# Six row buffers for P, a later output projection and earlier loads of the second group's weights in a fused attention and gMLP kernel

## The chip, the cores and the metric

The kernel runs on one core of one Trainium2 chip. The metric is the device time of one execution in microseconds (us); of several executions the median is given.

## The reference, cut to what matters

```python
# x: 2048 x 512; 32 query heads of 128, 8 key/value heads (groups) of 2048 keys; bf16
h = layernorm(x) * (1 + ca) + sa                     # sa, ca, ga, ... from silu(c) @ w_mod
q = (h @ wq)                                         # per group: 4 heads share one k and v
p = softmax(q @ k.T / sqrt(128)); o = p @ v
x = x + ga * (o @ wo)                                # output projection, summed over the groups
# then a second layernorm and a gMLP block (not touched by the change)
```

## The kernel before

The attention is cut into 128 **units**: 16 query tiles of 128 rows for each of 8 groups, four heads each. **Iteration** n computes the scores of unit n in eight slots (two 128x512 matmuls and one exponential of 128x1024 each), and beside them in the same slots the product with V (PV) of an earlier unit, the query projection of a later block and the output projection of a still earlier unit. In this way TensorE always has work while ScalarE computes exponentials.

Units come in two forms. "By columns": scores come out with keys on the partitions, so P is at once what PV wants. "By rows" (every second unit from 8 to 120): scores come out with queries on the partitions, ScalarE sums the rows as it goes, VectorE scales them, and P goes through a DMA transpose on the Sync queue into the place where PV, three iterations later, reads it. Each of the four heads of such a unit has one row buffer of 4 KB per partition, used again by the next unit by rows, two iterations later.

```python
    pn = [win_t[:, r * SK : (r + 1) * SK] for r in range(REP - 1)]
    pn.append(wmod_a[:].rearrange("p k n -> p (k n)")[:, 0:SK])   # the fourth row buffer
    ...
    TURN_A, TURN_B = 2 * CT, NU - CT - 2                # 8 and 122

    def by_rows(u):
        return TURN_A <= u < TURN_B and u % 2 == 0

    def pv_at(u):
        return u + 3 if by_rows(u) else u + 1
    ...
            nc.scalar.activation(                        # in qk(u, i): hh, half = divmod(i, 2)
                out=pn[hh][:, half * HK : (half + 1) * HK], in_=s_ps[:], func=ACT.Exp,
                scale=inv_sqrt_dh, accum_out=rsums[u][:, i : i + 1],
            )
    ...
    def turn_rows(u, hh):
        ...                                              # tot = sum of the two halves; rinv = 1 / tot
        nc.vector.tensor_scalar(out=pn[hh], in0=pn[hh], scalar1=rinv, scalar2=None, op0=ALU.mult)
        nc.sync.dma_start_transpose(out=pTs[u][:, :, hh * P : (hh + 1) * P], in_=pn[hh])
```

The output oT of a unit by columns goes through a DMA transpose too, on the same Sync queue, and the output projection reads it two iterations after PV. The loads of a group's weights stand in the order of the GpSimd queue. The slot given with `at` sets only that order: an instruction goes out as soon as the queue reaches it and its buffers are free, which can be many iterations ahead of its slot.

```python
    for g in range(1, HKV):
        it = (g - 1) * NT
        at(it + 7, 4, lambda g=g: load_wq(g, nc.gpsimd))
        at(it + 9, 5, lambda g=g: load_k(g))             # a DMA transpose from DRAM, on Sync
        at(it + 11, 4, lambda g=g: load_v(g))
        at(it + 13, 4, lambda g=g: load_wo(g, nc.gpsimd))
    ...
        wos = [u for u in (it - 7, it - 5, it - 3) if 0 <= u < NU and pv_at(u) + 2 == it]
```

## Time and profile before

| | kernel before |
|---|---|
| time, median of the first 3 runs | 1315.53 us (1315.16 to 1317.28) |
| span in the profile | 1313.5 us |
| TensorE busy | 1293.9 us, 99% |
| ScalarE busy | 1109.7 us, 84% |

The prediction works out what bounds this kernel and where TensorE waits.

### The profile page before, as it was taken

The page shows a single profiled execution, that of the slowest core. Times are in us where ns is not written, and L with a number is a line of the kernel's source. Part 1 is how long each engine was busy: PE and PEld are TensorE (multiplying, and loading weights), DVE is VectorE, ACT ScalarE, POOL GpSimd, SP SyncE. Part 2 cuts the span into 40 slices and gives each one's busy share as a digit, 9 for nine tenths or more (in the row PEclk, how much of TensorE's full clock was granted, in tenths as well). Part 3 has the DMA queues.
Part 4 walks back from the last instruction along what each step waited for, and adds up shares of the span by engine and source line. Part 5 has one row for each costly group of instructions (what it writes and reads, how often), then busy time and mean ns, then how long its engine had stood idle before and what let it go on. Part 6 is the DMA issues. An engine that isn't in the chain of part 4 may idle for free.

```text
span 1313.5 us, 24523 instructions
## 1 busy us (share of the span) xinstructions
PE 1293.9 (99%) x9452; PEld 740.6 (56%) x9623; DVE 683.1 (52%) x1675; ACT 1109.7 (84%) x1517; POOL 53.9 (4%) x96
## 2 busy tenths in 40 slices
PE   9999999999999999999999999999999999999998
PEld 5665555555555555555555555555555556644445
DVE  6644454444455544445454544444555686784444
ACT  7899999999999999999999999999999998650000
POOL 1110000000000000000000000000000011120000
PEclk9999999999999999999999999999999999999999
DMA  6479787978777777778786868687766673264300
GB/s 181 106 119 187 127 154 127 150 135 154 151 145 145 135 145 141 140 140 165 136 157 124 160 124 157 130 156 149 147 126 127 122 135 85 52 140 99 75 20 27
DMA packets 592172, 170.53 MB, mean 130 GB/s; under 512 B 581712, under 2 KB 588112, under 8 KB 592048
## 3 DMA queue, kind: packets, MB, share of 16 engines
q1 hardware_dynamic: 585024, 149.74, 62.3%
q0 software_dynamic: 4432, 16.91, 4.6%
q10 hardware_dynamic: 2592, 2.23, 0.5%
q8 instruction: 77, 1.26, 0.4%
q14 instruction: 47, 0.39, 0.1%
HBM read 21.89 MB, written 2.10 MB: 18 GB/s over the span
## 4 chain that ended last, share of the span: by engine, by line
PE 97%; DMA 1%; issue 1%; DVE 0%; ACT 0%; ACTq 0%; DVEq 0%
PE o_ps L1076 20%; PE s_ps L1020 19%; PE s_ps L1001 15%; PE o_ps L1055 15%; PE misc L1108 8%; PE misc L944 8%; PE misc L1433 7%; PE s_ps L1267 2%; PE s_ps L1306 2%; PE o_ps L1454 1%; DMA wsp<-wmod_a 1%; PE s_ps L1454 0%; DMA wmod_a<-in_w_mod_dram 0%; PE misc L854 0%; PE o_ps L785 0%
## 5 line engine op out<-in xcount | busy, mean ns | idle before, releaser
L1027 ACT ACTIVATE pT<-s_ps 128x1024 bf16<-128x1024 f32 x560 | 567.9, 1025 | 33.1 <-PE s_ps L1020 10.4
L1076 PEld LDWEIGHTS <-pT 128*128 128x128 bf16 x4480 | 299.5, 98 | 130.8
L1008 ACT ACTIVATE win_sb<-s_ps 128x1024 bf16<-128x1024 f32 x342 | 349.9, 1024 | 7.4 <-PE s_ps L1001 1.1
L1076 PE MATMUL o_ps<-v,pT 128*128 128x129 bf16 x4480 | 344.9, 220 | 1.2
L1020 PE MATMUL s_ps<-qT,kT 128*128 128x512 bf16 x1136 | 337.8, 379 | 2.9 <-ACT wmod_a L1008 1.3
L1001 PE MATMUL s_ps<-kT,qT 128*128 128x512 bf16 x889 | 266.5, 379 | 3.0
L1108 PE MATMUL misc<-wo_g,oT 128*128 128x512 bf16 x465 | 176.5, 380 | 1.7 <-DMA oT<-onorm 1.1
L1020 PEld LDWEIGHTS <-kT 128*128 128x128 bf16 x1136 | 110.1, 98 | 115.9 <-issue 4.5
L944 PE MATMUL misc<-hT,wq_g 128*128 128x512 bf16 (+2 forms) x480 | 172.7, 371 | 0.8
L1055 PEld LDWEIGHTS <-v 128*128 128x128 bf16 x912 | 89.2, 98 | 107.6
L955 DVE CAST qT<-misc 128x512 bf16<-128x512 f32 x125 | 85.7, 686 | 120.7 <-PE misc L944 120.6
L1064 DVE CAST oT<-o_ps 128x512 bf16<-128x512 f32 x57 | 39.4, 692 | 191.7 <-PE o_ps L1055 154.6
L1055 PE MATMUL o_ps<-wsp,v 128*128 128x512 bf16 x442 | 132.7, 379 | 0.6
L1042 DVE TENSOR_SCALAR win_sb<-win_sb,rall 128x2048 bf16<-128x2048 bf16 x171 | 128.8, 753 | 6.2 <-DVE rall L1041 0.3
L1055 PE MATMUL o_ps<-pT,v 128*128 128x512 bf16 x426 | 128.6, 379 | 0.6
L1001 PEld LDWEIGHTS <-qT 128*128 128x128 bf16 x912 | 89.1, 98 | 60.1 <-issue 0.2
L1008 ACT ACTIVATE wmod_a<-s_ps 128x1024 bf16<-128x1024 f32 x114 | 116.6, 1023 | 2.6 <-DMA wsp<-wmod_a 1.3
L1038 DVE TENSOR_TENSOR tot<-rs 128x1 f32<-128x1 f32 x228 | 35.2, 154 | 132.8 <-ACT win_sb L1008 131.6
L1433 PE MATMUL misc<-wsp,z 128*128 128x512 bf16 (+2 forms) x554 | 100.4, 336 | 0.5 <-issue 0.2
L1433 PEld LDWEIGHTS <-z 128*128 128x128 bf16 x560 | 50.6, 98 | 48.5
L1121 DVE TENSOR_TENSOR xacc<-misc,xacc 128x512 f32<-128x512 f32 x112 | 76.2, 680 | 0.0
L944 PEld LDWEIGHTS <-wq_g 128*128 128x128 bf16 x528 | 50.4, 98 | 29.3 <-issue 0.4
(107 smaller groups left out, 734.5 us busy)
## 6 DMA issues: line engine op xcount, KB each, us to landing
wq_g<-in_A_wq_dram POOLq DMA_DIRECT2D x7, 512.0 KB, 6.3
v<-in_A_v_cache_dram POOLq DMA_DIRECT2D x7, 512.0 KB, 6.2
wo_g<-in_A_wo_dram POOLq DMA_DIRECT2D x7, 512.0 KB, 4.3
wsp<-in_w_mod_dram POOLq DMA_DIRECT2D x1, 2048.0 KB, 10.3
out_dram<-yout ACTq DMA_DIRECT2D x16, 128.0 KB, 1.7
win_sb<-in_B_w_in_dram POOLq DMA_DIRECT2D x1, 1792.0 KB, 7.9
x_sb<-in_A_x_dram SPq DMA_DIRECT2D x3, 512.0 KB, 5.7
wsp<-win_sb SPq DMA_TRANSPOSE x87, 4.4
```

Of the source, the lines that this page charges most:

```text
L944: nc.tensor.matmul(ps[0][:, o0 : o0 + n], lhsT=wqs[g][:, dt, hh * DH : (hh + 1) * DH], rhs=hTs[ch][:, dt, c0 : c0 + n], start=(dt == 0), s ...
L955: nc.vector.tensor_copy(out=dst, in_=src)
L1001: nc.tensor.matmul(s_ps[:, c * 512 : (c + 1) * 512], lhsT=qTs[b][:, hh, jj * P : (jj + 1) * P], rhs=groups[g]["kT"][:, k0 : k0 + 512], sta ...
L1008: nc.scalar.activation(out=pn[hh][:, half * HK : (half + 1) * HK], in_=s_ps[:], func=ACT.Exp, scale=inv_sqrt_dh, accum_out=rsums[u][:, i : ...
L1020: nc.tensor.matmul(s_ps[:, h * 512 : (h + 1) * 512].rearrange("p (r q) -> p r q", r=REP), lhsT=groups[g]["kT"][:, kt * P : (kt + 1) * P], ...
L1027: nc.scalar.activation(out=pTs[u][:, 2 * i : 2 * i + 2, :], in_=s_ps[:].rearrange("p (k q) -> p k q", k=2), func=ACT.Exp, scale=inv_sqrt_dh,)
L1042: nc.vector.tensor_scalar(out=pn[hh], in0=pn[hh], scalar1=rinv, scalar2=None, op0=ALU.mult)
L1055: nc.tensor.matmul(o_pss[u][:], lhsT=groups[g]["v1"][:, kt, 0:DH], rhs=pTs[u][:, kt, :], start=(kt == 0), stop=(kt == NKT - 1),)
L1076: nc.tensor.matmul(o_ps[:, hh % 2, 0 : DH + 1], lhsT=pTs[u][:, kt, hh * P : (hh + 1) * P], rhs=groups[g]["v1"][:, kt, 0 : DH + 1], start=( ...
L1108: nc.tensor.matmul(X_ps[:], lhsT=oTs[u][:, hh, :], rhs=groups[g]["wo"][:, hh, :], start=(hh == 0), stop=(hh == REP - 1),)
L1121: nc.vector.tensor_tensor(out=xaccs[j][:], in0=X_ps[:], in1=xaccs[j][:], op=ALU.add)
L1433: nc.tensor.matmul(g_ps[:, :n], lhsT=z2[:, st, f * P : (f + 1) * P], rhs=wsp[t][:, st, c0 : c0 + n], start=(st == 0), stop=(st == NT - 1 a ...
```

## The change

Its intent: P by rows shall find a free buffer (a ring of six in place of four); the projection shall not wait for oT (one iteration later for units 8 to 121, with five oT buffers in place of three); and the loads for group 1 shall be out of the way before the transposes of P begin (at slot 2 of iteration 5, ahead of the modulation rows, which go to DRAM and back and behind which they stood).

```diff
--- before.py
+++ after.py
@@ -659,6 +659,7 @@
 
     pn = [win_t[:, r * SK : (r + 1) * SK] for r in range(REP - 1)]
     pn.append(wmod_a[:].rearrange("p k n -> p (k n)")[:, 0:SK])
+    pn += [early.tile([P, SK], BF16, name=f"pn{k}", bufs=1) for k in range(2)]
     wmod_b = wspp.tile([P, NDT * 4 * D], BF16, name="wsp")[:].rearrange(
         "p (k n) -> p k n", k=NDT
     )
@@ -731,7 +732,7 @@
             nc.sync.dma_start(
                 out=v1[:, NKT // 2 : NKT, 0:DH], in_=v_dram[:, 0, NKT // 2 : NKT]
             )
-        groups[g]["v1"] = v1
+        groups.setdefault(g, {})["v1"] = v1
 
     def load_wo(g, engine):
         wo_g = late.tile([P, REP, D], BF16, name="wo_g")
@@ -741,7 +742,7 @@
     def load_k(g):
         kT = early.tile([P, SK], BF16, name="kT")
         nc.sync.dma_start_transpose(out=kT[:], in_=A_k_cache[0, g])
-        groups[g] = dict(kT=kT)
+        groups.setdefault(g, {})["kT"] = kT
 
     nc.gpsimd.memset(mhalf[:], -0.5)
     make_identity(nc, ident[:])
@@ -970,6 +971,9 @@
     def pv_at(u):
         return u + 3 if by_rows(u) else u + 1
 
+    def wo_at(u):
+        return pv_at(u) + (3 if TURN_A <= u < TURN_B else 2)
+
 
     users, homes = dict(pT0=-2, pT1=-1, wsp=CT + 2), {}
     for u in range(NU):
@@ -1006,7 +1010,7 @@
                     stop=True,
                 )
             nc.scalar.activation(
-                out=pn[hh][:, half * HK : (half + 1) * HK],
+                out=rows_of(u, hh)[:, half * HK : (half + 1) * HK],
                 in_=s_ps[:],
                 func=ACT.Exp,
                 scale=inv_sqrt_dh,
@@ -1031,6 +1035,9 @@
             scale=inv_sqrt_dh,
         )
 
+    def rows_of(u, hh):
+        return pn[((u - TURN_A) // 2 * REP + hh) % len(pn)][:, 0:SK]
+
     def turn_rows(u, hh):
         c0 = u * REP + hh
         rs, rinv = rsums[u], rall[:, c0 : c0 + 1]
@@ -1039,12 +1046,9 @@
             out=tot[:], in0=rs[:, 2 * hh : 2 * hh + 1], in1=rs[:, 2 * hh + 1 : 2 * hh + 2], op=ALU.add
         )
         nc.vector.reciprocal(out=rinv, in_=tot[:])
-        nc.vector.tensor_scalar(
-            out=pn[hh], in0=pn[hh], scalar1=rinv, scalar2=None, op0=ALU.mult
-        )
-        nc.sync.dma_start_transpose(
-            out=pTs[u][:, :, hh * P : (hh + 1) * P], in_=pn[hh]
-        )
+        rows = rows_of(u, hh)
+        nc.vector.tensor_scalar(out=rows, in0=rows, scalar1=rinv, scalar2=None, op0=ALU.mult)
+        nc.sync.dma_start_transpose(out=pTs[u][:, :, hh * P : (hh + 1) * P], in_=rows)
 
     def pv_rows(u, i, n):
 
@@ -1060,7 +1064,7 @@
                 stop=(kt == NKT - 1),
             )
         if i == n - 1:
-            oTs[u] = late.tile([P, REP, P], BF16, name="oT", bufs=3)
+            oTs[u] = late.tile([P, REP, P], BF16, name="oT", bufs=5)
             nc.vector.tensor_copy(
                 out=oTs[u][:], in_=o_pss[u][:].rearrange("p (r q) -> p r q", r=REP)
             )
@@ -1092,7 +1096,7 @@
                 op=ALU.mult,
             )
         if i == NSLOT - 1:
-            oTs[u] = late.tile([P, REP, P], BF16, name="oT", bufs=3)
+            oTs[u] = late.tile([P, REP, P], BF16, name="oT", bufs=5)
             nc.sync.dma_start_transpose(
                 out=oTs[u][:], in_=onorms[u][:].rearrange("p r d -> p (r d)")
             )
@@ -1250,10 +1254,10 @@
         at(NU + 1 + st // 4, 2 * (st % 4), lambda st=st: load_wsp(wsp[0], 0, st))
     for g in range(1, HKV):
         it = (g - 1) * NT
-        at(it + 7, 4, lambda g=g: load_wq(g, nc.gpsimd))
         at(it + 9, 5, lambda g=g: load_k(g))
-        at(it + 11, 4, lambda g=g: load_v(g))
-        at(it + 13, 4, lambda g=g: load_wo(g, nc.gpsimd))
+        at(*((5, 2) if g == 1 else (it + 7, 4)), lambda g=g: load_wq(g, nc.gpsimd))
+        at(*((5, 2) if g == 1 else (it + 11, 4)), lambda g=g: load_v(g))
+        at(*((5, 2) if g == 1 else (it + 13, 4)), lambda g=g: load_wo(g, nc.gpsimd))
 
 
     zs = {}
@@ -1356,7 +1360,7 @@
             z2p = fast.enter_context(tc.tile_pool(name="z2p", bufs=1))
             zs["z2"] = z2p.tile([P, NT, FH], BF16, name="z2")
         pvs = [u for u in (it - 5, it - 3, it - 1) if 0 <= u < NU and pv_at(u) == it]
-        wos = [u for u in (it - 7, it - 5, it - 3) if 0 <= u < NU and pv_at(u) + 2 == it]
+        wos = [u for u in range(max(it - 6, 0), min(it - 2, NU)) if wo_at(u) == it]
         wf = [fn for u in wos for fn in wo_proj(u)]
         for i in range(NSLOT):
             for fn in later.pop((it, i), []):
```

## The prediction

> **What bounds the kernel now.** The first thing read was the busy shares and, with them, the shares of the chain that ended last.
>
> ```profile
> PE 1293.9 (99%) x9452; PEld 740.6 (56%) x9623; DVE 683.1 (52%) x1675; ACT 1109.7 (84%) x1517; POOL 53.9 (4%) x96
> PE 97%; DMA 1%; issue 1%; DVE 0%; ACT 0%; ACTq 0%; DVEq 0%
> ```
>
> TensorE is busy for 1293.9 of 1313.5 us and is 97% of the chain. A busy TensorE may still be idling inside its matmuls, so I checked the step from one matmul to the next. In the middle of the attention, two 128x512 matmuls start every 0.43 us, 216 ns each, and eight 128x129 ones take 0.46 us, 57 ns each. That is the rate of a pipeline that never waits. I then took, for every pair of neighbouring matmuls in the whole trace, the distance of their starts less the usual step of that shape (a distance that is one whole step too long is a missing record and left out). The excess, by stretch, is 2.9 us in the first 20 us, 3.5 us from 80 to 120 us, 0.7 us from 260 to 280 us, 1.9 us after 1300 us, and below 0.2 us in each other stretch of 20 us; 7.6 us in all after small negative terms. The change touches neither the start nor the end of the program, so it can win at most 3.5 + 0.7 = 4.2 us of 1315.5. The view of busy time by stretch shows the same two places, 1.8 us short and 0.5 us short of their neighbours:
>
> ```profile
> 100.00:120.00 20.00, 18.00 (x135) 10.06 (x136) 7.60 (x21) 17.66 (x30) 0.00 (x0) 1.00 1.07 199
> 120.00:140.00 20.00, 19.84 (x157) 11.75 (x158) 10.64 (x28) 19.56 (x31) 0.00 (x0) 1.00 0.77 120
> ...
> 260.00:280.00 20.00, 19.31 (x145) 11.10 (x146) 10.30 (x27) 18.58 (x29) 0.00 (x0) 1.00 0.74 131
> ```
>
> The columns after the length are busy us of TensorE, weight loads, VectorE, ScalarE, GpSimd, then the clock, the DMA share and GB/s. The DMA share of 1.07 beside 0.77 says what is special about the first place. The timeline there, in order of time:
>
> ```profile
> 81.86 0.76 POOL L720 DMA_DIRECT2D wq_g<-in_A_wq_dram  x1
> 82.75 1.18 POOL L728 DMA_DIRECT2D v<-in_A_v_cache_dram  x1
> 83.90 0.78 POOL L738 DMA_DIRECT2D wo_g<-in_A_wo_dram  x1
> ...
> 85.97 12.32 SPq L1045 DMA_TRANSPOSE wsp<-win_sb  x3
> 98.45 1.58 SPq L1096 DMA_TRANSPOSE oT<-onorm  x1
> 100.14 3.76 SPq L1045 DMA_TRANSPOSE wsp<-wmod_a  x1
> 103.94 2.73 SPq L743 DMA_TRANSPOSE kT<-in_A_k_cache_dram  x1
> ...
> 104.27 0.39 PE L1108 MATMUL misc<-wo_g,oT 128*128 128x512 bf16 x1 [1.06 <-DMA oT<-onorm]
> 107.57 1.02 ACT L1008 ACTIVATE wmod_a<-s_ps 128x1024 bf16<-128x1024 f32 x1 [1.27 <-DMA wsp<-wmod_a]
> 108.74 0.59 PE L1020 MATMUL s_ps<-qT,kT 128*128 128x512 bf16 x2 [0.78 <-ACT wmod_a L1008]
> ```
>
> (A unit is 128 query rows of the four heads of one group; iteration n computes the scores of unit n in eight slots.) The second group's weights, 1.5 MB, leave the GpSimd queue at 82 to 85 us, because they stand behind the round trip of the modulation rows through DRAM. From 86 us unit 8, the first unit by rows, sends its P through DMA transposes on the Sync queue. Three of them occupy that queue for 12.3 us (7.1 us at 609 us), so unit 7's oT goes out at 98.45, lands 5.8 us later (median 2.7) and TensorE waits 1.06 us for it. Unit 8's fourth transpose, behind oT, lands at about 107.5; ScalarE may not overwrite that row buffer with unit 10's P before, waits 1.27 us, and TensorE runs out of score banks for 0.78 us.
>
> The second place is the same overwrite without the other wait:
>
> ```profile
> 264.00 1.02 ACT L1008 ACTIVATE wmod_a<-s_ps 128x1024 bf16<-128x1024 f32 x1 [1.03 <-PE s_ps L1001]
> 265.16 0.59 PE L1020 MATMUL s_ps<-qT,kT 128*128 128x512 bf16 x2 [0.54 <-ACT wmod_a L1008]
> ```
>
> The view blames TensorE for the first wait, but the scores of that slot started at 262.26 and were done by 262.85; by 264.00 TensorE was writing the next bank. I read it as the wait for the transpose that still read the fourth row buffer.
>
> **What the Trainium skill says.** "Perfetto Trace Analysis", Identifying the Most-Contended Engine, warns that matmul busy time is no measure of the distance to the peak; hence the check of steps. "TensorE: Matmul & The Clock Gate", Back-to-back issue gap, gives N / 2.4 + 2.5 ns for an isolated gap (215.8 for 512, 56.3 for 129) and 131 ns for N=512 in a stream with weight loads. The trace has 216 and 57 ns in just such a stream: it agrees with the first and not with the second, so I count on no faster rate. "DMA: Bandwidth & Descriptors", Issuing engines are not separate DMA queues, says that transfers started from Scalar, Sync and GpSimd run on the same 16 engines and interleave; the slowed transposes beside the GpSimd loads agree, with 302 and 276 GB/s at 86 to 88 and 90 to 92 us against about 140 in the steady stretch.
>
> **The change, part by part.** No instruction is added or taken: all matmuls, activations and transposes stay, so the 1300 us of TensorE work stays.
>
> *Earlier loads.* In the built program the three loads of group 1 now stand right after the last LN1 statistics on GpSimd, ahead of the modulation rows. That instruction ended at 59.7 us, so they go out at about 60 to 62.5 and, at the 5 to 6 us that they took, are gone by 70. The DMA share is 0.47 from 60 to 80 us, so there is room. Unit 8's three transposes then need 7 to 8 us of the queue instead of 12.3, oT goes out some 4 us earlier, lands near 98, and is wanted at 103.0. Worth: the excess at that matmul is 1.22 us, less some 0.07 that stays: 1.15 us.
>
> *Ring of six.* Unit 10's heads use buffers 4, 5, 0, 1, so its third and fourth head overwrite heads that unit 8 sent two heads earlier, some 4 us more slack than now. Both ScalarE waits go: 0.94 us of excess at 108.74 and 0.70 us at 265.16, together 1.64 us. Elsewhere this overwrite costs TensorE nothing now, so there is no more to win.
>
> *Output projection one unit later.* From unit 8 on it moves from PV plus two units to PV plus three. No later projection waits for oT in the trace, and unit 7, whose projection waits, is not moved. What it does is leave iteration 12 without projection. A slot by rows is 0.43 + 0.46 = 0.89 us on TensorE without fill and 1.10 us with one more matmul, and ScalarE needs about 1.00 us (starts at 99.99 and 100.99). So four slots of iteration 12 become bound by ScalarE. In iteration 8, where the same happens, two of four slots are hidden by the two score banks and two lose 0.12 us. I charge 0.25 us. The four matmuls come back in iteration 126, where they fill TensorE.
>
> Sum: -1.15 - 1.64 + 0.25 = -2.5 us; 1315.5 becomes 1313.0 us, or a span of about 1311.0.
>
> **The rivals.** *The stalls move.* The new loads meet the four hT transposes (60.7 to 65.9) and the oT transposes behind them. If these slip by 6 us, hT lands at about 79 instead of 73 (estimated from the DMA share, which ends at 76) and VectorE, which wants it at 78.7, waits; oT of unit 4 is wanted at about 78 and has more than 5 us to spare. Against it: 76 to 82 us is empty of DMA in the trace. Cost if true: up to 1 us, which makes 1314.0. *The congestion stays.* Group 2's wq still leaves at 97.7 us (it waits for the last use of its buffer) and the K cache is still transposed near 100, so oT or P could be late all the same; the earlier load then wins nothing of the 1.15 us: 1314.1. *VectorE at the end.* Iterations 125 and 126 now both carry two projections of the last group. One costs four operations of 0.69 us and a short one, 2.9 us, so 126 has 5.9 us of these, 1.2 us of PV eviction and 2.8 us of LN2 turns: 9.9 us in an iteration of about 8.9. That makes VectorE late by 1 to 2 us; two banks each of o_ps and misc cover four slots, 4.4 us, so I expect no stall. If one comes: +0.5 to 1 us. *More is won than the trace shows.* Three runs spread from 1315.16 to 1317.28; if the late overwrite hits other groups in other runs, the ring removes that too, and the median falls by 3 to 3.5 us, to 1312.0 or so.
>
> **Range and chances.** All rivals together lie between 1311.5 (everything of the 4.2 us is won) and 1315. The steady stretch has nothing to win, and 2% is 26 us, six times everything that the change can reach; a loss of 26 us would need a new stall of 0.2 us in every unit. So within 2% is nearly sure.
>
> **What would show it.** TensorE busy from 100 to 120 us should rise from 18.0 to 19.5 or more, from 260 to 280 us from 19.3 to 19.8. The wait of the output projection for oT at 104 us and both waits of ScalarE should be gone, the three transposes of unit 8 should take 7 to 9 us on the Sync queue, and the loads should stand at 60 us. Iteration 12 should show steps of 1.00 us in its last slots. Wrong would be a wait of TensorE at 60 to 82 or 1105 to 1125 us of over 0.3 us, or any wait in the steady stretch, above all for P by rows.

## More of the kernel before

In the list of DMA issues (what is loaded, queue, count, KB each, median us from issue to landing) the loads of wo_g land after 4.3 us:

```profile
wo_g<-in_A_wo_dram POOLq DMA_DIRECT2D x7, 512.0 KB, 4.3
```

and the view of the tile oT from 60 to 82 us, cut to its last line, gives the time that the two oT transposes issued there took (6.3 us is that of unit 4, 7.4 that of unit 5):

```profile
DMA to landing us min/median/max: 6.3/6.8/7.4
```

## The result and the profile after

| | before | after |
|---|---|---|
| time, median of 4 runs each | 1316.28 us (1315.16 to 1317.28) | 1314.93 us (1314.00 to 1315.48) |
| span in the profile | 1313.5 us | 1311.9 us |

The ratio is 0.9989 with a 95% interval of 0.9972 to 1.0007. A ratio is the mean time of one kernel's runs over that of the other's of the same rounds, so it is not quite the ratio of the medians that I quote. The time is 1.9 us above the predicted 1313.0 us, at the upper end of the 1311.5 to 1315 us that the prediction gave for all its rivals together; 1.35 us were won by the medians where 2.5 us had been forecast.

Since the order of the score matmuls is the same in both kernels, the starts of the iterations (first weight load of a unit's scores) can be set side by side; this table is worked out from the two traces:

| stretch | before | after | difference |
|---|---|---|---|
| start of the program to unit 0 | 10.38 | 10.68 | +0.30 |
| iteration 7 | 8.81 | 9.70 | +0.89 |
| iteration 10 | 9.70 | 8.47 | -1.23 |
| iteration 11 | 8.29 | 7.21 | -1.08 |
| iteration 12 | 8.86 | 8.35 | -0.51 |
| units 29 to 40 (the place at 264 us) | 96.53 | 95.83 | -0.70 |
| iteration 126 | 8.00 | 8.81 | +0.81 |
| everything else | | | -0.09 |
| sum | | | -1.61 |

The 0.30 us at the start are chance: the first 20 us are untouched by the change, and across all profiles unit 0 starts anywhere from 10.2 to 11.3 us. Nearly all other iterations agree to 0.01 us (iteration 13 differs by 0.04). So the gains came, and one loss of 0.89 us with them. The view of busy time by stretch of the changed kernel (columns as in the prediction) shows both:

```profile
60.00:80.00 20.00, 19.28 (x204) 13.04 (x202) 7.88 (x22) 17.39 (x17) 5.19 (x8) 1.00 1.07 129
...
100.00:120.00 20.00, 19.99 (x161) 11.65 (x159) 8.46 (x25) 20.00 (x33) 0.00 (x0) 1.00 1.01 184
...
260.00:280.00 20.00, 20.00 (x159) 11.74 (x158) 10.12 (x25) 19.29 (x31) 0.00 (x0) 1.00 0.80 138
```

From 100 to 120 us TensorE is busy for 19.99 us where it was 18.00, from 260 to 280 for 20.00 where it was 19.31. (Some matmul records were missing in the trace before, so a full stretch shows 19.84 there and 20.00 here.) But from 60 to 80 us it now misses 0.7 us, at a DMA share of 1.07; before, this stretch had 19.79 us at a share of 0.47. The timeline there:

```profile
60.01 0.81 POOL L721 DMA_DIRECT2D wq_g<-in_A_wq_dram  x1
...
61.07 1.31 POOL L729 DMA_DIRECT2D v<-in_A_v_cache_dram  x1
62.38 0.76 POOL L739 DMA_DIRECT2D wo_g<-in_A_wo_dram  x1
```
```profile
61.01 5.72 SPq L845 DMA_TRANSPOSE hT<-xn  x4
66.82 18.21 SPq L1100 DMA_TRANSPOSE oT<-onorm  x3
87.17 9.08 SPq L1051 DMA_TRANSPOSE wsp<-win_sb  x3
96.35 1.63 SPq L1100 DMA_TRANSPOSE oT<-onorm  x1
98.08 1.79 SPq L1051 DMA_TRANSPOSE wsp<-wmod_a  x1
```
```profile
79.35 1.38 DVE L814 TENSOR_SCALAR hT<-hT,modc 128x512 bf16<-128x512 bf16 x4 [0.28 <-DMA hT<-xn]
79.63 0.39 PE L1112 MATMUL misc<-wo_g,oT 128*128 128x512 bf16 x1 [0.72 <-DMA oT<-onorm]
```

The loads go out at 60 us, as meant, and meet the four transposes of hT (the transposed output of the first layernorm, which the query projection reads). The first oT behind them, that of unit 4, leaves at 66.82 us, only 0.9 us later than before, but it is slow in flight; its projection in iteration 7 waits for it. The view of the tile oT from 60 to 82 us ends with

```profile
DMA to landing us min/median/max: 5.7/9.2/12.8
```

12.8 us where the same transpose took 6.3 us before; 66.82 plus 12.8 is 79.6, the moment at which the projection starts. Unit 8's three transposes then hold the queue for 9.08 us, not 12.32, unit 7's oT leaves at 96.35, not 98.45, and nothing waits in iterations 10 and 11.

Iteration 12 lost its projection, and its last slots are paced by ScalarE, as predicted; the starts of its score matmuls are 1.0 us apart at 0.89 us of work:

```profile
121.27 0.59 PE L1005 MATMUL s_ps<-kT,qT 128*128 128x512 bf16 x2
...
122.27 0.59 PE L1005 MATMUL s_ps<-kT,qT 128*128 128x512 bf16 x2
...
123.27 0.59 PE L1024 MATMUL s_ps<-qT,kT 128*128 128x512 bf16 x2
```

One more line has changed that I had not thought of, in the list of DMA issues:

```profile
wo_g<-in_A_wo_dram POOLq DMA_DIRECT2D x7, 512.0 KB, 10.6
```

The loads of wo_g land after 10.6 us, not 4.3. A load of wo_g goes out when the last projection of the group two before it is done; this is now one iteration later, and falls beside the transposes of P.

### The profile page after: what moved, and what is told of

Read it like the earlier page. It is cut to its first block, busy times and chain, and to the rows that moved or that the text cites. A ratio compares the mean times of both kernels' runs of the same rounds, so it can differ in the third digit from the quotient of the medians.

```text
span 1311.9 us, 24470 instructions
## 1 busy us (share of the span) xinstructions
PE 1304.1 (99%) x9623; PEld 741.0 (56%) x9623; DVE 682.6 (52%) x1675; ACT 1111.1 (85%) x1517; POOL 54.0 (4%) x96
## 4 chain that ended last, share of the span: by engine, by line
PE 98%; DMA 1%; DVE 0%; ACT 0%; SPq 0%; issue 0%; DVEq 0%
PE o_ps L1080 19%; PE s_ps L1024 18%; PE s_ps L1005 15%; PE o_ps L1059 15%; PE misc L1112 8%; PE misc L945 8%; PE misc L1437 7%; PE s_ps L1271 2%; PE s_ps L1310 2%; PE o_ps L1458 1%; DMA oT<-onorm 1%; PE o_ps L786 1%; PE s_ps L1458 1%; PE misc L855 0%; PE o_ps L945 0%; DVE hT L814 0%
## 5 line engine op out<-in xcount | busy, mean ns | idle before, releaser
L1031 ACT ACTIVATE pT<-s_ps 128x1024 bf16<-128x1024 f32 x560 | 568.5, 1024 | 34.4 <-PE s_ps L1024 11.3
L1005 PE MATMUL s_ps<-kT,qT 128*128 128x512 bf16 x912 | 271.2, 379 | 0.0
L1012 ACT ACTIVATE win_sb<-s_ps 128x1024 bf16<-128x1024 f32 x228 | 233.3, 1024 | 3.4
L1112 PE MATMUL misc<-wo_g,oT 128*128 128x512 bf16 x512 | 194.1, 379 | 0.7 <-DMA oT<-onorm 0.7
L945 PE MATMUL misc<-hT,wq_g 128*128 128x512 bf16 (+2 forms) x520 | 187.0, 371 | 0.1
L1012 ACT ACTIVATE pn<-s_ps 128x1024 bf16<-128x1024 f32 x152 | 155.4, 1023 | 2.0 <-ACT wmod_a L1012 0.3
L1059 PE MATMUL o_ps<-wsp,v 128*128 128x512 bf16 x464 | 137.3, 379 | 0.0
L1059 PE MATMUL o_ps<-pT,v 128*128 128x512 bf16 x448 | 133.2, 379 | 0.0
L1050 DVE TENSOR_SCALAR win_sb<-win_sb,rall 128x2048 bf16<-128x2048 bf16 x114 | 85.9, 753 | 4.2 <-DVE rall L1048 0.3
L1012 ACT ACTIVATE wmod_a<-s_ps 128x1024 bf16<-128x1024 f32 x76 | 77.8, 1024 | 0.0
## 6 DMA issues: line engine op xcount, KB each, us to landing
wo_g<-in_A_wo_dram POOLq DMA_DIRECT2D x7, 512.0 KB, 10.6
```

What stands on the lines that cost most here:

```text
L945: nc.tensor.matmul(ps[0][:, o0 : o0 + n], lhsT=wqs[g][:, dt, hh * DH : (hh + 1) * DH], rhs=hTs[ch][:, dt, c0 : c0 + n], start=(dt == 0), s ...
L1005: nc.tensor.matmul(s_ps[:, c * 512 : (c + 1) * 512], lhsT=qTs[b][:, hh, jj * P : (jj + 1) * P], rhs=groups[g]["kT"][:, k0 : k0 + 512], sta ...
L1012: nc.scalar.activation(out=rows_of(u, hh)[:, half * HK : (half + 1) * HK], in_=s_ps[:], func=ACT.Exp, scale=inv_sqrt_dh, accum_out=rsums[u ...
L1031: nc.scalar.activation(out=pTs[u][:, 2 * i : 2 * i + 2, :], in_=s_ps[:].rearrange("p (k q) -> p k q", k=2), func=ACT.Exp, scale=inv_sqrt_dh,)
L1050: nc.vector.tensor_scalar(out=rows, in0=rows, scalar1=rinv, scalar2=None, op0=ALU.mult)
L1059: nc.tensor.matmul(o_pss[u][:], lhsT=groups[g]["v1"][:, kt, 0:DH], rhs=pTs[u][:, kt, :], start=(kt == 0), stop=(kt == NKT - 1),)
```

## The experiments

My theory after the first look: the saving was right, and 0.9 us of it was given back through the new wait for the oT of unit 4, which comes from loads and transposes in flight together. The rivals: the missing part is scatter; the wait at 107 us was itself only a result of the late loads; the later projection does more than the profile shows. The first two groups of four ran on one chip, the third on another. Medians, in us:

| run | what it has | median (lowest to highest) | runs | ratio to before (95%) |
|---|---|---|---|---|
| before, groups 1 and 2 | | 1315.13 (1314.36 to 1318.65) | 12 | |
| after_again | the whole change | 1313.70 (1313.35 to 1314.73) | 5 | 0.9982 (0.9968 to 0.9996) |
| loads_only | earlier loads | 1314.98 (1314.19 to 1318.72) | 6 | 1.0000 (0.9984 to 1.0016) |
| ring_only | ring of six | 1315.10 (1314.94 to 1315.36) | 5 | 0.9992 (0.9979 to 1.0006) |
| wo_only | later projection | 1319.84 (1317.77 to 1321.17) | 5 | 1.0024 (1.0010 to 1.0039) |
| no_wo | ring and earlier loads | 1315.77 (1314.81 to 1317.65) | 5 | 1.0001 (0.9986 to 1.0015) |
| gap | ring, loads at 50 us | 1313.51 (1312.82 to 1313.61) | 5 | 0.9979 (0.9965 to 0.9992) |
| wo_gated | later projection, wo_g loads held back | 1316.49 (1315.68 to 1319.03) | 6 | 1.0005 (0.9991 to 1.0018) |
| no_loads | ring and later projection | 1315.72 (1314.50 to 1317.28) | 5 | 0.9995 (0.9981 to 1.0010) |
| before, group 3 | | 1315.21 (1314.69 to 1319.88) | 11 | |
| after_third | the whole change | 1315.86 (1314.45 to 1319.34) | 6 | 1.0005 (0.9989 to 1.0020) |
| quiet | ring, loads at 50 us, wq loads held back | 1313.26 (1313.00 to 1313.88) | 6 | 0.9981 (0.9969 to 0.9993) |
| wq_gated | wq loads held back, nothing else | 1315.04 (1314.08 to 1315.58) | 6 | 0.9993 (0.9982 to 1.0005) |
| wo_from4 | the whole change, later projection from unit 4 | 1313.08 (1312.62 to 1314.10) | 6 | 0.9980 (0.9968 to 0.9992) |

All gave correct results. "Excess" below is, as in the prediction, the distance from one matmul's start to the next beyond the usual step.

### after_again: the changed kernel as the yardstick

> The changed kernel once more, as the yardstick for the others. Theory: the saving of 2.5 us was given back in part by a new wait of TensorE for the oT of unit 4 at about 79 us (0.7 to 0.9 us), because the earlier loads slow that transpose. So the wait is there again in this profile, and the time is 1.3 to 1.7 us under the kernel before. Rival (the missing part is scatter of the start of the program): the wait is absent or under 0.3 us in this profile and the time differs from the kernel before by 2.2 us or more.

The profile has the wait again: an excess of 0.79 us at 78.6 us, before the projection of unit 4. The time is 1.47 us under the kernel before by the medians. The theory's figures hold. The rival does not: unit 0 started 0.13 us earlier than in the first profile of the changed kernel, so scatter of the start is small beside the wait.

### loads_only: the earlier loads alone

```diff
-        at(it + 7, 4, lambda g=g: load_wq(g, nc.gpsimd))
+        at(*((5, 2) if g == 1 else (it + 7, 4)), lambda g=g: load_wq(g, nc.gpsimd))   # v, wo alike
```

> The kernel before with nothing but the earlier loads of group 1. Theory: the wait for the oT of unit 7 at 104 us goes (-1.2 us), the new wait for the oT of unit 4 comes (+0.9 us), and both waits of ScalarE for the fourth row buffer (near 107 and 264 us) stay, since only the ring takes them: 0.3 us under the kernel before. Rival: the wait near 107 us was only a result of the late loads, so it goes here too and only the one at 264 us stays: 1.4 us under the kernel before.

The wait for the oT of unit 7 is gone, the one for the oT of unit 4 is there with an excess of 1.12 us. In the place where ScalarE waited 1.27 us for the fourth row buffer it now goes from one activation to the next:

```profile
105.53 1.06 ACT L1008 ACTIVATE win_sb<-s_ps 128x1024 bf16<-128x1024 f32 x1
106.44 0.25 ACT L1008 ACTIVATION_READ_ACCUMULATOR win_sb<-s_ps 128x1 f32 x1
106.60 1.02 ACT L1008 ACTIVATE wmod_a<-s_ps 128x1024 bf16<-128x1024 f32 x1
```

So the rival was right: that wait was a result of the late loads, and needs no ring. The wait at 264 us is absent in this profile as well, though nothing in this kernel could have removed it, which was the first sign that it does not occur in every run. The profile's span is 1.3 us under that of before; by the medians 0.15 us is won and by the means (the ratio of 1.0000) nothing: two of six runs took over 1318 us.

### ring_only: the ring of six alone

```diff
+    pn += [early.tile([P, SK], BF16, name=f"pn{k}", bufs=1) for k in range(2)]
...
+    def rows_of(u, hh):
+        return pn[((u - TURN_A) // 2 * REP + hh) % len(pn)][:, 0:SK]
```

> The kernel before with nothing but the ring of six row buffers. Theory: both waits of ScalarE go (-1.1 and -0.7 us), the wait for the oT of unit 7 at 104 us stays at about 1.1 us: 1.8 us under the kernel before. Rival (the wait of ScalarE near 107 us was hidden behind the wait for oT, or is not an overwrite at all): 0.7 us or less under the kernel before.

Both waits of ScalarE are gone, and the wait for the oT of unit 7 is there (for the one at 264 us this shows nothing: the wq load before it took 1.5 us from first to last packet in this profile, 8.2 us in that of the kernel before):

```profile
104.50 0.39 PE L1112 MATMUL misc<-wo_g,oT 128*128 128x512 bf16 x1 [1.01 <-DMA oT<-onorm]
```

So the ring, too, is enough for the wait at 107 us: loads or ring, either one takes it, and their savings there must not be added. The median is only 0.03 us under that of before, not 1.8. The profiled run has a wait which no theory had, with an excess of 1.14 us; whether the other four have one too is not on record:

```profile
823.27 0.59 PE L1059 MATMUL o_ps<-pT,v 128*128 128x512 bf16 x2 [0.98 <-DVE rall L1045]
```

The view blames a reciprocal on VectorE. PV reads nothing of it; what PV reads is P after its transposes, and in that stretch (812 to 822 us) the DMA moved 77 to 106 GB/s, at a share of 1.1 to 1.8, where bursts of transposes elsewhere show about 200 at a share of 1.1. P was late. What the ring did change is the scatter: five runs within 0.4 us, beside 4.3 us among the runs of before.

### wo_only: the later projection alone

```diff
-        wos = [u for u in (it - 7, it - 5, it - 3) if 0 <= u < NU and pv_at(u) + 2 == it]
+        wos = [u for u in range(max(it - 6, 0), min(it - 2, NU)) if wo_at(u) == it]
```

> The kernel before with nothing but the later output projection. Theory: no projection from unit 8 on ever waited, so nothing is won; iteration 12 loses its four projection matmuls and becomes bound by ScalarE for some slots: 0.2 to 0.4 us slower than the kernel before, all three old waits still there. Rival (the later projection takes a wait away that the profile hides): 0.5 us or more faster.

(The function wo_at and the five oT buffers come with this edit, as in the change.) Both were wrong: 4.7 us slower by the medians, and every run at least 2.6 us over the median of before. The profile has the waits to overwrite the fourth row buffer at 263, 631, 771 and 824 us, with an excess of 1.7, 0.6, 0.9 and 2.2 us. The last one:

```profile
825.40 1.02 ACT L1010 ACTIVATE wmod_a<-s_ps 128x1024 bf16<-128x1024 f32 x1 [2.54 <-DMA pT<-wmod_a]
```
```profile
828.00:830.00 2.00, 2.00 (x6) 0.61 (x5) 0.70 (x1) 1.46 (x2) 0.00 (x0) 0.50 1.02 191
```

The second line is the view by stretch shortly after. It shows a granted clock of 0.50: after the wait of 2 us TensorE ran at half speed, for 3.4 us by the clock records of the trace, which costs half of it, 1.7 us, on top of the wait itself.

Where do the waits come from? I took, from the DMA packets of the GpSimd queue, the time from first to last packet of each load of 512 KB. In the kernel before, the wo_g loads take 2.2 to 3.6 us. In wo_only, those of groups 3 to 7 take 4.2, 8.2, 9.0, 9.8 and 5.1 us, and three wq loads take 6.7 to 9.1 us. The waits at 631 and 771 us stand just behind two of the slow wo_g loads (617 to 626 and 756 to 766 us), those at 263 and 824 us behind two slow wq loads (253 to 261 and 814 to 823 us). During such a load the transposes are slow as well: the mean time of a 256-byte packet on the Sync queue is 77 to 84 ns in the stretches at 617, 756 and 814 us, beside 21 to 22 ns in the same stretches of the kernel before (the median stays at 18 ns). And in the kernel before, the wait at 264 us stood behind the only wq load that was slow there (254.7 to 262.9 us). So a load beside the stream of P transposes goes along with both being slow; the next experiment, and two later ones, move the loads.

### wo_gated: later projection, wo_g loads held back

```diff
+        if g > 1:        # a small instruction that waits for a projection one iteration later
+            at(it + 13, 3, lambda: gate(xaccs[1][:, 0:1]))
         at(it + 13, 4, lambda g=g: load_wo(g, nc.gpsimd))
```

Here gate(src) is one GpSimd tensor_scalar of 128x1 from src into a scratch tile.

> The kernel with only the later projection, which was 4.7 us slower than the kernel before, plus one small GpSimd instruction ahead of each later wo_g load that holds it back by one more iteration, out of the stream of P transposes. Theory: the 4.7 us came from the wo_g loads (8 to 10 us in flight beside the transposes, which then reach their buffers late, so that ScalarE waits to overwrite them); held back they take 2 to 4 us, and the waits near 631 and 771 us are gone: within 1 us of the kernel before plus 0.3 us. Rival (the later projection itself delays the transposes or VectorE): still 3 us or more over the kernel before.

The wo_g loads take 2.2 to 2.9 us from first to last packet, and land after 5.3 us at the median (10.2 in wo_only):

```profile
wo_g<-in_A_wo_dram POOLq DMA_DIRECT2D x7, 512.0 KB, 5.3
```

The waits at 631 and 771 us are gone and 3.35 of the 4.7 us are won back: 1.36 us over the kernel before, where the theory wanted at most 1.3 and the rival at least 3. So at least a good part of the cost of wo_only came from the place of the wo_g loads, and not from the projections. How much is not settled: in the profile of wo_only the two waits behind wo_g loads are 1.4 us, the two behind wq loads 3.9 us with 1.7 us of half clock, and wo_gated does not hold back the wq loads. The size of the gain rests on the medians of 5 and 6 runs. What does not rest on them: wo_g loads of groups 4 to 6 took 6.3 to 9.7 us, 18 of 18, in the six profiles with the later projection and no gate, and 2.2 to 3.7 us, 24 of 24, in the others, this one included. What is left is a wq load, which nothing held back: from 392.2 to 402.1 us, and behind it ScalarE waits for the row buffer again, and the clock drops again.

```profile
403.47 1.02 ACT L1010 ACTIVATE wmod_a<-s_ps 128x1024 bf16<-128x1024 f32 x1 [2.60 <-DMA pT<-wmod_a]
```
```profile
406.00:408.00 2.00, 2.00 (x6) 0.73 (x5) 0.75 (x1) 0.95 (x2) 0.00 (x0) 0.50 0.80 156
```

### no_wo: ring and earlier loads, projection as before

> Ring of six and earlier loads, output projection as in the kernel before. Theory: the later projection only costs (0.3 us in iterations 12 and 126), and with the ring its other effect, the load of each later group's wo_g falling into the stream of P transposes, is absorbed. So the wo_g loads of groups 4 to 6 take 2 to 4 us again instead of 8 to 9, the wait for the oT of unit 4 near 79 us stays (0.7 to 1.1 us), and the time is 0.2 to 0.5 us under that of the changed kernel, 1.8 us under the kernel before. Rival (the later projection is what makes the ring work): 0.5 us or more over the changed kernel, with waits for P in the steady stretch.

The wo_g loads are fast again (4.3 us to landing), there is no wait after 130 us, and yet the time is 2.1 us over after_again. All of it stands in one line:

```profile
81.39 0.39 PE L1112 MATMUL misc<-wo_g,oT 128*128 128x512 bf16 x1 [2.73 <-DMA oT<-onorm]
```

The wait for the oT of unit 4 is 2.7 us here. My figure for the time was wrong, since I had taken this wait to be 0.7 to 1.1 us; the rival's figure was met, but not its reason, for its waits in the steady stretch are absent. The iterations from 8 on differ from those of after_again by what the later projection costs, and by nothing else.

### gap: the loads at 50 us

```diff
+    def gate_loads():                                    # reads a result of unit 3
+        ve = stat.tile([P, CT], FP32, name="ve_ln1")
+        nc.gpsimd.tensor_scalar(out=ve[:, :1], in0=rall[:, 3 * REP : 3 * REP + 1],
+                                scalar1=LN_EPS, scalar2=None, op0=ALU.add)
...
+        at(4, 4, gate_loads)                             # then wq, v, wo of group 1 at (4, 5)
```

> Ring of six, projection as before, and the three loads of group 1 held back by a small GpSimd instruction that reads a result of unit 3, so that they go out at about 50 us, where no DMA runs, instead of 60 us beside the hT and oT transposes. Theory: the wait for the oT of unit 4 goes (it came from loads and transposes in flight together), the wait for the oT of unit 7 stays away: no step of TensorE over 0.2 us too long from 60 to 82 us, 0.7 to 1.1 us under the kernel with the same ring and the loads at 60 us. Rival (what delays that oT is its place behind the four hT transposes on the Sync queue, not the loads): the wait stays and the two kernels are within 0.3 us.

```profile
49.16 0.23 POOL L1251 TENSOR_SCALAR ve_ln<-rall 128x1 f32<-128x1 f32 x1 [10.89 <-DVE rall L1091]
49.34 0.81 POOL L721 DMA_DIRECT2D wq_g<-in_A_wq_dram  x1
```
```profile
DMA to landing us min/median/max: 5.8/6.9/8.0
```

The loads go out at 49 us, the oT transposes between 60 and 82 us take at most 8.0 us (14.3 in no_wo), and no step from 60 to 82 us is too long. Against no_wo, the same kernel with the loads at 60 us, 2.26 us are won by the medians, more than expected because of the size of the wait there. The place on the Sync queue is unchanged, so the rival falls: it is the loads. All profiles together say the same: the oT of unit 4 landed after 10.9 to 14.3 us in the six with loads at 60 us and after 5.7 to 7.5 us in the eight with loads at 50 or 82 us. All five runs lie within 0.8 us. What remains in the profile is one wait for P of 0.56 us at 820 us, behind a wq load that took from 810.0 to 818.6 us.

### no_loads: ring and later projection, loads where they were

> The changed kernel with the loads of group 1 where they were. Theory: the wait for the oT of unit 7 near 104 us is back (1.1 to 1.2 us), the wait for the oT of unit 4 near 79 us is gone (0.7 to 0.9 us), nothing else moves: 0.2 to 0.5 us over the changed kernel, about 1.2 us under the kernel before. Rival (the earlier loads also spare waits later on): 1 us or more over the changed kernel.

The wait for the oT of unit 4 is gone and the one for unit 7 is back (excess 1.45 us), and beside it there is one for the oT of unit 6 of 1.02 us, in iteration 9, and one for P of 0.46 us at 265 us. The time is 2.0 us over after_again, so my figure of 0.2 to 0.5 was too small and the rival's was met, though not for its reason, that earlier loads spare waits later on: loads at 82 to 96 us can delay more than one transpose. Of the 2.0 us, 0.8 lie outside the spans, whose medians are 1312.8 and 1311.6 us; why this kernel spends more time there (2.5 to 3.1 us a run, 2.1 to 2.3 in after_again) is not known. By the same reading, loads beside transposes cost a varying amount, here more than in the profile of the kernel before.

### after_third: the changed kernel once more, on the other chip

> The changed kernel again, for comparison within this group of runs. Theory: a wait for the oT of unit 4 near 79 us of 0.7 to 2.9 us (it was 0.8, 1.1 and 2.9 us in the profiles with loads at 60 us), differing from run to run, so the runs spread over 1 us or more; about 1.4 us under the kernel before. Rival: the same wait as in the first profile, 0.9 us, in every run, and no more scatter than 0.5 us.

The wait for the oT of unit 4 has an excess of 2.20 us, and there is one for P of 0.71 us at 544 us and one of 0.42 us at 49 us. Six runs spread over 4.9 us, so the first half of the theory holds. The time is 0.65 us over the median of before, so its second half, a gain of 1.4 us, does not. Taken together, the 15 runs of the changed kernel have a mean of 1315.10 and the 27 of the kernel before 1315.88: 0.8 us, 0.06%, with both scattering over more than 5 us. By the scatter of these runs that difference is uncertain by about 1 us either way (95%), so a gain of the whole change is not shown beyond the noise.

### quiet: all loads out of the way

```diff
+        if g > 2:        # waits for the projection of iteration 16 (g - 2) + 11
+            at(it + 6, 0, lambda: gate(xaccs[6][:, 0:1]))
         at(*((4, 5) if g == 1 else (it + 7, 4)), lambda g=g: load_wq(g, nc.gpsimd))
```

> The kernel with ring and loads at 50 us, and in addition the wq loads of groups 3 to 7 held back by a small GpSimd instruction that reads a finished projection, so that they go out at the start of the next even iteration, before its P transposes. Theory: of the waits in the steady stretch what is left comes from wq loads that are in flight beside the P transposes for 8 to 10 us; held back they take 2 to 4 us each, and no step of TensorE from 130 to 1090 us is over 0.2 us too long: a span of about 1310.6 us, a time of 1312.7 us, at least 1 us under the changed kernel. Rival (late P has another cause): waits for P or for a row buffer still appear in the steady stretch, or the wq loads still take over 6 us.

From 130 to 1090 us there is not one step of over 0.1 us too much, and the wq loads of groups 3 to 7 take 1.7 to 2.4 us. The span is 1311.3 us instead of 1310.6, because the program started 0.87 us later than in the profile before (unit 0 at 11.25 us); without that the sum was right. Its six runs lie between 1313.00 and 1313.88, all below the fastest run of the kernel before in that group (1314.69): this version beats both kernels. On its chip it is 2.6 us under the changed kernel by the medians.

### wq_gated: nothing but the held-back wq loads

> The kernel before with nothing but the held-back wq loads of groups 3 to 7; no ring, loads of group 1 and projection as they were. Theory: the wait of ScalarE to overwrite the fourth row buffer at 264 us, and like ones that differ from run to run, come from wq loads in flight beside the P transposes; held back they are gone without a ring. The waits at 104 and 107 us stay. So a span near 1312.7 us, runs within 1 us of each other, where the kernel before spread over 4 us. Rival (four buffers are too few for the transposes as such): waits for the fourth row buffer still appear after 130 us, and the spread is that of the kernel before.

The wq loads take 1.7 to 2.2 us, and no wait appears after 130 us, with four row buffers. The waits at 104 us (excess 0.72) and 107 us (0.96) are there as expected. The span is 1312.9 us, expected 1312.7. The six runs spread over 1.5 us, the runs of before in the same group over 5.2, though without its slowest run over 1.2. One profile without a wait would prove little, for loads_only had none either, without this edit. Three things together make the case. In all profiles each wait of over 0.25 us after 130 us stands behind a GpSimd load that took 8.2 us or more. Of the 60 wq loads of groups 3 to 7 that nothing held back, 13 took over 6 us; all ten that were held back, here and in quiet, took 1.7 to 2.4 us. And here the waits are gone with four row buffers. So the waits for the row buffers in the steady stretch come with slow loads beside the P transposes, and holding the loads back takes them away without a ring; that the scatter goes for the same reason is likely, but rests on few runs.

### wo_from4: the later projection from unit 4 on

```diff
-        return pv_at(u) + (3 if TURN_A <= u < TURN_B else 2)
+        return pv_at(u) + (3 if CT <= u < TURN_B else 2)
```

> The changed kernel with the later projection from unit 4 on instead of unit 8, so that the projection that waits for the oT of unit 4 comes one iteration (8.8 us) later. Theory: that wait goes (0.8 to 2.9 us), iteration 11, bound by ScalarE, gets the projection of unit 7, and nothing else changes: 1 us or more under the changed kernel. Rival (TensorE then waits for something else that the same loads delay, such as hT at 79 us): a wait of over 0.5 us between 75 and 90 us, and less than 0.4 us won.

The loads are at 60 us and oT is late as before, but nobody wants it yet: no step between 60 and 82 us is too long, and there is no wait for hT or anything else up to 90 us beyond the known ScalarE pace (0.12 us a slot). 1313.08 us by the median, 2.8 us under the changed kernel on the same chip. Iteration 11 became 0.7 us longer than in the changed kernel, as expected. So one bound of the change, moved from unit 8 to unit 4 where the wait was, gives more than the 1 us that this edit was to win (after_third itself had a larger wait there than usual, and others besides). Against the kernel before it is 2.1 us by the medians, where the prediction had 2.5.

## Why the prediction was wrong, point by point

- **The bound, and that within 2% was sure:** right. The steady iterations agree to 0.01 us.
- **Earlier loads, -1.15 us:** right as a term, -1.23 in the profile. But the loads were not "gone by 70", at "the 5 to 6 us that they took": in the trace before, the three landed 6.6, 9.8 and 10.3 us after issue, beside transposes of P, and beside those of hT after 4.2, 9.1 and 13.2 us, the last at 75.5 us. The wait for oT, below, comes from this.
- **Ring of six, -0.94 and -0.70 us:** the sizes were met, -1.08 (which has the end of the first wait in it) and -0.70 in the profile, the reason only half. Loads_only shows that the earlier loads take the first wait without any ring, so this was one saving with two sufficient causes. The -0.70 has luck in it: loads_only, without a ring, has the same -0.70. In the profile of the changed kernel the wq load there was slow (7.7 us) and nothing waited, which fits the ring; but in no_loads, with the ring and a load of 9.3 us, PV waited 0.46 us in the same place.
- **Later projection, +0.25 us:** the direct part was right, +0.30: iteration 12 became 0.51 us shorter although 0.86 us of matmuls left it, and iteration 126 longer by 0.81. What I missed is that the projection also releases the buffer of wo_g. Moved by one iteration, it sends these loads into the stream of P transposes (10.6 us to landing, not 4.3). With four row buffers the later projection made the kernel 4.7 us slower; with the ring no wait stands behind these loads in any of five profiles.
- **"oT of unit 4 is wanted at about 78 and has more than 5 us to spare": the step that failed.** I had seen the collision, named it as a rival, guessed a slip of 6 us, and then dismissed it for oT with a spare time of a little over 5 us, which leaves no margin. The traces show both: before, this oT landed at 72.3 us and was wanted at 78.4, a spare of 6.1 us; in the changed kernel it landed at 79.6, 7.3 us later: 6.4 us longer in flight (12.8 instead of 6.3) and 0.9 us later in its issue, 0.3 us of this being the later start of the program. TensorE waited 0.7 us (0.89 us of the iteration). For hT the same rival was right in time, landing at 79.3 us where it said about 79, but VectorE waited only 0.28 us for it. Nor is the size fixed: the excess was 0.88, 0.79, 1.12, 2.89 and 2.20 us in the five profiles with loads at 60 us and the projection of unit 4 in its old place. With -2.5 us and this term of 0.9 the sum is -1.6, and so is the difference of the two spans, with some luck: the terms as measured give -1.8, and 0.2 us of chance, mostly at the start, makes it -1.6.
- **"Elsewhere this overwrite costs TensorE nothing now, so there is no more to win":** wrong, and the last rival had half of it right: the late overwrite does hit other groups in other runs, but the ring does not take it all away, for with six buffers PV still waited for P in four profiles (0.46 to 1.14 us), and the median did not fall by 3 us. One profile shows one run. The wait at 264 us was one draw of a collision that comes and goes with the wq loads; loads_only had none, wo_gated had one at 402 us that cost 4 us with the half clock.
- **VectorE at the end:** right to be dismissed; no step from 1100 to 1125 us is too long.

What stays open is why a load and a stream of transposes slow each other so much in one case and not in another. In the traces, the 13 slow wq loads of groups 3 to 7 all sent their first packet 1.9 to 3.0 us after issue and were then 6.4 to 9.9 us long; those that started after 3.1 us or more took at most 4.6 us, and so did the few that started after 1.5 us, as all those held back did. So it seems to matter whether the load gets in before the last transposes of a burst are through. This was seen, not tested; nor was anything else that differs between these moments, such as the work of VectorE while a load is being issued.

## What to carry to other kernels

Before moving a load to a place where the DMA share looks low, list every transfer in flight there with its time to landing and the moment at which its result is wanted, and compare the slip with the spare time in the same unit; a mean share of 0.47 says nothing about a transfer with 5 us to spare. A move that changes when a buffer is released moves the loads that wait for that buffer, so follow it to the end. Where a load goes out "as soon as it can", a small instruction that waits for the right event is a cheap way to put it into a quiet place. The runs of gap and quiet, which do this, spread by 0.8 and 0.9 us where those of before spread by 4.3 and 5.2; ring_only spread by 0.4 us without it, so what sets the scatter is not shown.

## What the Trainium skill lacked or had wrong

- "DMA: Bandwidth & Descriptors", Rules for kernel authors, says that a DMA transpose next to ordinary DMAs needs nothing. As for correctness this agrees with the runs, all of which were correct. What it lacks is the cost: beside three GpSimd loads of 512 KB the oT transpose of unit 4 landed after 10.9 to 14.3 us instead of 5.7 to 7.5; beside one such load the packets of the P transposes took 77 to 84 ns in the mean instead of 21 to 22, and the load itself 6 to 10 us where most take 1.5 to 4.
- The same page, Issuing engines are not separate DMA queues, says that transfers interleave. The runs agree. What it lacks is that the total rate can fall with it: in the slow stretches it was 77 to 106 GB/s, where bursts of transposes alone reach about 200.
- "TensorE: Matmul & The Clock Gate", HAM oscillation, gives the rule that TensorE must not idle for more than about 3.4 us. Here a wait of 2.0 and one of 2.1 us was followed by 3.413 us at half clock (wo_only at 828 us, wo_gated at 405 us); waits of 2.7 us (no_wo) and of 1.1 us (ring_only) were not. So the threshold is not a sure 3.4 us. The traces show more: every stretch at full clock lasted a whole multiple of 3.413 us (117, 142, 241, 265, 382 or 383 of them). I laid this grid over the matmul records, whose ends are modelled, and took the idle time of TensorE within each cell. All cells with 2.04 us or more of it, in the middle of the program and at its end, were followed by half clock, none with 1.5 us or less was; of the two between, 1.88 us (after_again, at the end) was and 1.98 us (after_third, at 78 to 81 us) was not. The 2.7 us of no_wo fell into two cells, 1.44 and 1.29 us.
- The same page, Back-to-back issue gap, gives 131 ns for a matmul with N=512 in a stream with weight loads. The steady stretch shows 216 ns for 512 and 57 ns for 129 columns, in a stream with weight loads, throughout; the formula that it gives for the isolated gap fits.
- No page has a word on the release of a wait being blamed on the wrong engine by the profile. Here PV at 823 us is put down to a VectorE reciprocal that it does not read, and the ScalarE wait at 264 us to TensorE.
